# Moving the branch to a general path ahead of the last two row groups of a projection

## The chip, the cores and the metric

The kernel runs on one core of one Trainium2 chip. The core has five engines that each run their own list of instructions in order: TensorE (PE in the profile, with its weight loads as PEld), VectorE (DVE), ScalarE (ACT), GpSimd (POOL) and SyncE (SP), which here only issues transfers. Sixteen DMA engines move data between the chip's memory (HBM) and the core's on-chip memories, SBUF and, for the results of TensorE, PSUM with eight banks. Engines wait for one another through counters (semaphores). The metric is the device time of one execution in microseconds (us), the median of several runs; a profiled execution gives the trace.

## The reference

Causal attention over a sliding window of 64 positions, and a SwiGLU feed-forward block behind it:

```
q, k, v: (8 batches, 8 heads, 576 positions, 64)
scores = q @ k^T / 8;  kept where 0 <= pos_q - pos_k < 64, else -1e9
attn   = softmax(scores);  x = attn @ v      -> 4608 tokens of 512
g   = x @ w_gate;  val = x @ w_val           (512 -> 1536)
out = (silu(g) * val) @ w_out                (1536 -> 512), float32
```

## The kernel before, in words

The kernel computes in bfloat16 with float32 sums. It cuts the 4608 tokens into NT = 9 tiles of 512. Eight tiles are positions 0 to 511 of one batch each; the tile LAST = 7 collects positions 512 to 575 of all batches. The tile handled last, t = 8, is batch 7, tokens 4032 to 4543.

A tile goes through attention (scores, weights, totals, the mix with v, each with its helper), whose result is xT[t], transposed; then gate_value, twelve times, once for each 128 of the 1536 hidden features: eight products into two banks, SiLU on ScalarE, and a product on VectorE into hT[t] (line 467). hT[t] has shape 128 x 12 x 512: feature within a chunk, chunk, token. The projection takes a row group s, that is 128 of the 512 tokens, and sums twelve products over the chunks: `hT[t][:, c, P * s:P * s + P]` is the stationary operand and `wo[:, c, :]` the moving one (project_part, line 482). project_end copies the bank to a tile os_ and SP issues the transfer to the output. The loop over t puts the projection of tile t - 1 in among the attention of tile t. For the last tile it stands alone behind the loop (lines 986 to 988): row groups 0, 1 and 2 through project into banks 5, 7 and 4, and row group 3 through project_last, in two parts of 384 and 128 columns with a copy and a transfer each.

The fast path does not subtract the row maximum before the exponential. So it surveys its sums: fifty-six columns of `spread` hold totals and extents, survey (line 542) asks which lie within a bound, and tally (line 549) counts the partitions on which all do. Line 982 loads that count into a register of each engine. The If on line 989 then runs the general path where the count is below 128: general_attention once for each of 64 batch and head pairs, which keeps the maximum and writes x to a scratch tensor x_all in HBM, and general_ffn once for each 128 tokens, which reads x_all, computes the block anew and overwrites the output. Both issue their transfers on ScalarE's queue. Each engine takes the branch for itself, at its place in its list. In the run the count is 128: no instruction of lines 554 to 661 is in the trace.

The order of instructions on every engine is the order of the program text (a manual schedule). The framework adds the waits and the counters. Transfers issued by SP and ScalarE take eight counters in turn; in the trace they are 100, 103, 104, 105, 106, 107, 109 and 110. Where a branch does not run its body, its other arm adds to the counters what the body would have counted. Tiles of one tag share its buffers: os_ has four, and the tag hT of hpool has two.

```
    for s in range(3):
        project(NT - 1, s, bank[(5, 7, 4)[s]])
    project_last(NT - 1, 3)
    with tc.If(good < P, preferred_fallthrough_block=True):
```

Of the kernel before, what the change touches and what calls it, by code (L numbers as in the profile page):

```python
# [8 lines left out]
P = 128  # L9
FP32 = mybir.dt.float32  # L10
BF16 = mybir.dt.bfloat16
# [6 lines left out]
def kernel(  # L18
# [10 lines left out]
    nc = tc.nc  # L29
    S, D, H = 576, 64, 8  # L30
    NTOK, DFF, DM = 4608, 1536, 512
    NT = NTOK // 512
# [10 lines left out]
    hpool = ctx.enter_context(tc.tile_pool(name="hpool", bufs=2))  # L43
    ps = ctx.enter_context(tc.tile_pool(name="ps", bufs=1, space=PSUM))
    two = [ps.tile([P, 2, 512], FP32, name=f"two{i}") for i in range(2)]
    bank = [two[i][:, j] for i in range(2) for j in range(2)]
# [21 lines left out]
    scratch = ctx.enter_context(  # L68
        tc.tile_pool(name="scratch", bufs=1, space=bass.MemoryType.DRAM)
    )  # L70
    x_all = scratch.tile([H * D, NTOK], BF16, name="x_all")
    floor = cst.tile([P, 1], FP32, name="floor")
    LEAST, MOST = 2.0 ** -60, 2.0 ** 30
    columns_used = [0]
# [455 lines left out]
    def project_last(t, s):  # L530
        r0 = S * batch(t) + P * s
        os_ = fsb.tile([P, 512], FP32, name="os_", tag="os_", bufs=4)
        for f0, f1, o_ps in ((0, 384, bank[6]), (384, 512, bank[0])):
            for c in range(12):
                nc.tensor.matmul(  # L535
                    o_ps[:, 0:f1 - f0], hT[t][:, c, P * s:P * s + P], wo[:, c, f0:f1],
                    start=(c == 0), stop=(c == 11),
                )
            nc.vector.tensor_copy(os_[:, f0:f1], o_ps[:, 0:f1 - f0])
            nc.sync.dma_start(out[r0:r0 + P, f0:f1], os_[:, f0:f1])  # L540
# [13 lines left out]
    def general_attention(i):  # L554

        def rows(ap, lo, hi):
            return ap.rearrange("b h s d -> (b h) s d")[bass.ds(i, 1), lo:hi]

        plain, wide = {}, {}
        for n, src in (("q", q), ("k", k), ("v", v)):  # L560
            f = stage.tile([P, 6, D], FP32, name=n + "_g", tag=n, bufs=1 if n == "v" else 2)
            nc.gpsimd.memset(f[:], 0.0)
            lead = 0 if n == "q" else 64
            if lead:
                nc.scalar.dma_start(f[64:P, 0], rows(src, 0, 64).rearrange("o r d -> r (o d)"))
            else:
                nc.scalar.dma_start(f[0:64, 4], rows(src, 512, S).rearrange("o r d -> r (o d)"))
            c0 = lead // 64
            nc.scalar.dma_start(
                f[:, c0:c0 + 4], rows(src, lead, lead + 512).rearrange("o (c r) d -> r (o c) d", r=P)  # L570
            )
            plain[n] = epool.tile([P, 6, D], BF16, name=n + "_h", tag="both")
            nc.gpsimd.tensor_copy(plain[n][:], f[:])
        for n, b in (("q", 4), ("k", 5)):
            tp = bank[b].bitcast(BF16)
            for c in range(6):
                nc.tensor.transpose(tp[0:D, P * c:P * c + P], plain[n][:, c], identb[:])
            wide[n] = att.tile([P, 6 * P], BF16, name=n + "_w", tag="qT")
            nc.scalar.copy(wide[n][0:D], tp[0:D, 0:6 * P])
        W = P + 64  # L580
        s_ps = [two[c // 4][:, c % 4 // 2, c % 2 * W:c % 2 * W + W] for c in range(5)]
        for c in range(5):
            nc.tensor.matmul(
                s_ps[c], wide["q"][0:D, P * c:P * c + P], wide["k"][0:D, P * c:P * c + W]
            )
        s = room(2).rearrange("r a b -> r (a b)")[:, 0:5 * W].rearrange("r (c j) -> r c j", j=W)
        nc.scalar.activation(
            s[:, 0:4].rearrange("r (a c) j -> r a (c j)", a=2), two[0][:, :, 0:2 * W],
            AF.Copy, scale=0.125,
        )  # L590
        nc.scalar.activation(s[:, 4], s_ps[4], AF.Copy, scale=0.125)
        for sign, base in ((1, 64), (-1, -1)):
            nc.gpsimd.affine_select(
                out=s, in_=s, compare_op=ALU.is_ge, fill=-1e9,
                base=base, pattern=[[0, 5], [-sign, W]], channel_multiplier=sign,
            )
        nc.gpsimd.memset(s[:, 0, 0:64], -1e9)
        some = fsb.tile([P, 64], FP32, name="some", tag="fine", bufs=1)
        top, total = some[:, 0:5], some[:, 5:10]
        nc.vector.tensor_reduce(top, s, axis=mybir.AxisListType.X, op=ALU.max)  # L600
        nc.gpsimd.tensor_scalar(top, top, -1.0, 0.0, op0=ALU.mult, op1=ALU.add)
        for c in range(5):
            nc.scalar.activation(
                s[:, c], s[:, c], AF.Exp, bias=top[:, c:c + 1], accum_out=total[:, c:c + 1]
            )
        nc.gpsimd.tensor_scalar(total, total, 1.0, 1e-9, op0=ALU.mult, op1=ALU.add)
        nc.vector.reciprocal(total, total)
        e, p0, p1 = (t[:].rearrange("r s z -> r (s z)") for t in eb[0:3])
        e = e[:, 0:5 * W].rearrange("r (c j) -> r c j", j=W)
        nc.vector.tensor_mul(e, s, total.unsqueeze(2).to_broadcast([P, 5, W]))  # L610
        t0, t1 = bank[6].bitcast(BF16), bank[7].bitcast(BF16)
        for c in range(5):
            nc.tensor.transpose(t0[:, P * c:P * c + P], e[:, c, 0:P], identb[:])
            nc.tensor.transpose(t1[0:64, P * c:P * c + P], e[:, c, P:W], identb[:])
        nc.scalar.copy(p0[:, 0:5 * P], t0[:, 0:5 * P])
        nc.scalar.copy(p1[0:64, 0:5 * P], t1[0:64, 0:5 * P])
        o_ps = two[0][0:D].rearrange("r a b -> r (a b)")
        for c in range(5):
            cs = slice(P * c, P * c + P)
            nc.tensor.matmul(o_ps[:, cs], plain["v"][:, c], p0[:, cs], start=True, stop=False)  # L620
            nc.tensor.matmul(
                o_ps[:, cs], plain["v"][0:64, c + 1], p1[0:64, cs], start=False, stop=True
            )
        x_h = att.tile([P, S], BF16, name="x_h", tag="xT")
        nc.scalar.copy(x_h[0:D], o_ps[:, 0:S])
        nc.scalar.dma_start(
            x_all[bass.ds((i % H) * D, D), bass.ds((i // H) * S, S)], x_h[0:D]
        )

    def general_ffn(i):  # L630

        x_b = att.tile([P, 4, P], BF16, name="x_b", tag="xT")
        nc.scalar.dma_start(
            x_b[:], x_all[:, bass.ds(i * P, P)].rearrange("(c r) s -> r c s", r=P)
        )
        h_b = hpool.tile([P, DFF], BF16, name="h_b", tag="hT")
        h_t = hpool.tile([P, 12, P], BF16, name="h_t", tag="hT")
        for lo, hi, pair in ((0, 2, two), (2, 3, [bank[b].unsqueeze(1) for b in (4, 5)])):
            for w, ps_ in zip((wg, wv), pair):
                for f in range(lo, hi):  # L640
                    for c in range(4):
                        nc.tensor.matmul(
                            ps_[:, f - lo], x_b[:, c], w[:, c, 512 * f:512 * f + 512],
                            start=c == 0, stop=c == 3,
                        )
            sg, val = room(hi - lo), room(hi - lo)
            nc.scalar.activation(sg, pair[0][:], AF.Silu)
            nc.scalar.copy(val, pair[1][:])
            nc.gpsimd.tensor_mul(
                h_b[:, 512 * lo:512 * hi].rearrange("r (a f) -> r a f", f=512), sg, val  # L650
            )
        for b, c0 in ((6, 0), (7, 6)):
            tp = bank[b].bitcast(BF16)[:, 0:6 * P].rearrange("r (c s) -> r c s", s=P)
            for c in range(6):
                nc.tensor.transpose(tp[:, c], h_b[:, P * (c0 + c):P * (c0 + c) + P], identb[:])
            nc.scalar.copy(h_t[:, c0:c0 + 6], tp)
        for c in range(12):
            nc.tensor.matmul(bank[4], h_t[:, c], wo[:, c, :], start=c == 0, stop=c == 11)
        os_ = fsb.tile([P, 512], FP32, name="os_", tag="os_", bufs=4)
        nc.scalar.copy(os_[:], bank[4])  # L660
        nc.scalar.dma_start(out[bass.ds(i * P, P)], os_[:])

    def set_exp():
        nc.scalar.preload_act_table_set("natural_log_exp_and_others")
# [318 lines left out]
        count[0:1, 0:1], min_val=0, max_val=P,  # L983
        skip_runtime_bounds_check_because="a count of 128 partitions",
    )
    for s in range(3):
        project(NT - 1, s, bank[(5, 7, 4)[s]])
    project_last(NT - 1, 3)
    with tc.If(good < P, preferred_fallthrough_block=True):
        set_exp()  # L990
        with tc.For_i(0, 8 * H, 1) as b:
            general_attention(b)
        set_silu()
        with tc.For_i(0, NTOK // P, 1) as i:
            general_ffn(i)

# [1 line left out]
_INS = ['q', 'k', 'v', 'moe_w_gate', 'moe_w_val', 'moe_w_out']  # L998
# [26 lines left out]
```

## Time and profile before

| what | value |
|---|---|
| median of 3 runs | 323.33 us (323.15 to 324.28) |
| the profiled execution | 323.03 us |
| its span, first to last instruction | 321.3 us |
| granted TensorE clock over the span | 1.0 |
| TensorE, weight loads | 315.1 us (98%), 154.8 us (48%) |
| VectorE, ScalarE, GpSimd | 214.4, 208.7, 148.0 us |
| products of line 482, mean of one | 252, 379 ns |
| last copy of VectorE ends | 317.0 us |

The page of the profile counts as busy only what computes; register loads, branches, counter instructions and the issue of transfers are in the trace, with a q behind the engine's name (SPq, PEldq), and can be listed by the line that made them. The products of TensorE overlap: one of 512 columns lasts 379 ns, but the next starts 216 ns after it. "The chain" follows the work that ended last back to what released each step. The DMA view gives for any stretch the packets and their queue; the queues marked "instruction" carry the engines' own code.

### The profile page before, as it was taken

What the parts mean: (1) busy time and instruction counts of PE and PEld (TensorE: products, weight loads), DVE (VectorE), ACT (ScalarE), POOL (GpSimd) and SP (SyncE); (2) the same over time, 40 slices, a digit from 0 to 9 for tenths busy, and PEclk for the clock granted to TensorE, in tenths of its full rate; (3) what the DMA queues carried; (4) which work ended last, traced back from release to release, by engine and by line L of the source; (5) the groups of instructions that cost most, each with busy time, mean ns of one, the idle gap of its engine ahead of it and who ended that gap; (6) DMA issues with size and microseconds to landing.
All of it is one profiled execution on the core that took longest, in us unless ns stands there. A gap on an engine that the chain in (4) does not pass through costs nothing.

```text
span 321.3 us, 8212 instructions
## 1 busy us (share of the span) xinstructions
PE 315.1 (98%) x3298; PEld 154.8 (48%) x3298; DVE 214.4 (67%) x349; ACT 208.7 (65%) x327; POOL 148.0 (46%) x268
## 2 busy tenths in 40 slices
PE   8999999999999999999999999999999999999994
PEld 3544444445444644454445544554456444644442
DVE  4878846496676747684688657866785677744421
ACT  5967665768565875687467846694668565865500
POOL 4965656957557246741751099308665300000000
PEclk9999999999999999999999999999999999999999
DMA  7999999999799449974993379529997400021012
GB/s 251 204 196 198 207 147 229 201 194 132 153 193 181 49 114 179 194 79 106 162 199 41 80 115 116 65 62 143 181 185 100 107 0 0 4 92 43 0 44 92
DMA packets 83530, 40.45 MB, mean 126 GB/s; under 512 B 64161, under 2 KB 78753, under 8 KB 83489
## 3 DMA queue, kind: packets, MB, share of 16 engines
q0 software_dynamic: 51488, 22.59, 58.5%
q1 hardware_dynamic: 31456, 16.79, 22.7%
q8 instruction: 26, 0.43, 0.5%
q10 hardware_dynamic: 544, 0.52, 0.5%
q14 instruction: 16, 0.12, 0.1%
HBM read 53.02 MB, written 9.44 MB: 194 GB/s over the span
## 4 chain that ended last, share of the span: by engine, by line
PE 95%; ACT 2%; DMA 2%; ACTq 0%; DVE 0%; issue 0%
PE one L473 56%; PE one L482 17%; PE one L494 11%; PE two L293 3%; PE two L414 2%; PE one L449 2%; DMA k_f<-in_k_dram 2%; ACT eb L738 1%; PE two L336 1%; PE one L535 1%; PE two L449 1%; PE one L336 0%; ACT r L350 0%; ACT qk_b L724 0%; ACT r L353 0%; PE two L877 0%
## 5 line engine op out<-in xcount | busy, mean ns | idle before, releaser
L466 ACT ACTIVATE sg<-one 128x512 f32<-128x512 f32 x107 | 63.9, 597 | 80.5 <-PE one L473 65.5
L467 DVE TENSOR_TENSOR hT<-sg,one 128x512 bf16<-128x512 f32 x107 | 74.0, 692 | 57.5 <-PE one L473 53.8
L473 PE MATMUL one<-xT,wg 128*128 128x512 bf16 x416 | 106.8, 379 | 0.0
L473 PE MATMUL one<-xT,wv 128*128 128x512 bf16 x416 | 106.8, 379 | 0.0
L142 POOL DMA_DIRECT2D k_s<-in_k_dram x112 | 60.6, 570 | 26.5 <-DMA q_s<-in_q_dram 15.1
L473 PEld LDWEIGHTS <-wv 128*128 128x128 bf16 x416 | 40.7, 98 | 49.1
L473 PEld LDWEIGHTS <-wg 128*128 128x128 bf16 x416 | 40.6, 98 | 48.8
L482 PE MATMUL one<-wo,hT 128*128 128x512 bf16 x252 | 56.5, 379 | 0.0
L956 POOL COPY past<-xT 128x1 bf16<-128x1 bf16 x8 | 1.5, 192 | 88.1 <-DVE xT L430 88.1
L494 PE MATMUL one<-wo,hT 64*64 64x512 bf16 x672 | 40.0, 377 | 0.0
L482 PEld LDWEIGHTS <-hT 128*128 128x128 bf16 x252 | 23.8, 98 | 29.3 <-issue 2.0
L430 DVE TENSOR_TENSOR xT<-two,r 128x512 bf16<-128x512 f32 x34 | 21.2, 683 | 22.7 <-ACT r L353 22.7
L233 DVE STREAM_TRANSPOSE kT<-k_s 128x512 bf16<-128x512 bf16 x28 | 36.1, 1288 | 0.0
L753 ACT ACTIVATE eb<-eb 128x960 bf16<-128x960 bf16 (+1 forms) x32 | 32.0, 1001 | 0.0
L308 ACT ACTIVATE eb<-two 128x960 bf16<-128x960 f32 (+1 forms) x32 | 29.5, 974 | 3.0 <-PE two L293 2.9
L494 PEld LDWEIGHTS <-hT 64*64 64x64 bf16 x672 | 18.6, 107 | 13.7
L313 DVE TENSOR_TENSOR eb<-eb,mask 128x960 bf16<-128x960 bf16 (+1 forms) x32 | 21.0, 656 | 5.8 <-ACT eb L308 5.8
L223 DVE STREAM_TRANSPOSE qT<-q_s 128x512 bf16<-128x512 bf16 x32 | 22.2, 700 | 0.1
L353 ACT ACTIVATE r<-r 128x1024 f32<-128x1024 f32 (+1 forms) x20 | 19.2, 968 | 0.1
L318 DVE TENSOR_TENSOR both<-eb 128x512 bf16<-128x512 bf16 x32 | 13.6, 425 | 1.1
L107 POOL DMA_DIRECT2D q_s<-in_q_dram x24 | 13.1, 553 | 2.3 <-DMA v<-in_v_dram 1.3
L168 POOL DMA_DIRECT2D vb<-in_v_dram x16 | 11.1, 705 | 5.1 <-DMA wo<-in_moe_w_out_dram 3.5
(149 smaller groups left out, 272.9 us busy)
## 6 DMA issues: line engine op xcount, KB each, us to landing
k_s<-in_k_dram POOLq DMA_DIRECT2D x112, 56.0 KB, 5.0
q_s<-in_q_dram POOLq DMA_DIRECT2D x24, 248.0 KB, 6.0
v_f<-in_v_dram SPq DMA_DIRECT2D x40, 128.0 KB
wg<-in_moe_w_gate_dram POOLq DMA_DIRECT2D x5, 256.0 KB, 8.2
wv<-in_moe_w_val_dram POOLq DMA_DIRECT2D x5, 256.0 KB, 8.8
q_f<-in_q_dram SPq DMA_DIRECT2D x4, 256.0 KB
wo<-in_moe_w_out_dram POOLq DMA_DIRECT2D x2, 512.0 KB, 10.7
vb<-in_v_dram POOLq DMA_DIRECT2D x16, 64.0 KB, 6.2
```

Source lines behind the costliest of these rows:

```text
L142: nc.gpsimd.dma_start(k_s[p0:p0 + 32, g, :, 0:w], k[b, a:H:2, s:s + P].rearrange("u (r e) d -> r u (e d)", e=4) [:, :, 32 * c:32 * c + w],)
L223: nc.vector.transpose(queries[t][:, u, :].rearrange("r (e x) -> r e x", e=16), staged[t][0][:, u].rearrange("r (e d) -> r e d", d=D)[:, :, ...
L233: nc.vector.transpose(dst[:, u, :].rearrange("r (g x e) -> r g e x", g=4, e=4), k_s[:, :, u].rearrange("r g (e d) -> r g e d", d=D)[:, :, ...
L308: nc.scalar.activation(flat, s_ps[:].rearrange("r a b -> r (a b)")[:, 0:n], AF.Exp, scale=0.125)
L313: nc.vector.tensor_mul(flat, flat, mask[:].rearrange("r j c e y -> r (j c e y)")[:, 0:n])
L430: nc.vector.tensor_mul(x, o_ps, r)
L466: nc.scalar.activation(sg[:], g_ps[:], AF.Silu)
L467: nc.vector.tensor_mul(hT[t][:, m, :], sg[:], v_ps[:])
L473: nc.tensor.matmul(ps[:], w[:, c, P * m:P * m + P], xT[t][:, c, :], start=(c == 0), stop=(c == 3),)
L482: nc.tensor.matmul(o_ps[:], hT[t][:, c, P * s:P * s + P], wo[:, c, :], start=(c == 0), stop=(c == 11),)
L494: nc.tensor.matmul(tiles[s][half(y)], hT[t][half(x), c, r0:r0 + 64], wo[half(x), c, :], start=not back and c == 0, stop=bool(back) and c = ...
L753: nc.scalar.activation(flat, flat, AF.Copy, accum_out=extent())
```

## The change

The If moves up by two row groups. Ahead of it stay row groups 0 and 1 of the last tile; behind it come row group 2 through project and row group 3 through project_last. What they read, columns 256 to 511 of hT[NT - 1], must then hold the right values on either path, and so the general path no longer ends with the output alone:

- general_ffn takes its transposed hidden values h_t not as a tile of its own but as columns 384 to 511 of hT[NT - 1]. Before it overwrites them it copies them on ScalarE to columns 256 to 383. After the last two passes these hold the values of the last two groups of 128 tokens it handled.
- For these to be the tokens of row groups 2 and 3 (4288 to 4543), the groups are shifted by 64 tokens. x_all has 64 more columns; general_attention writes each batch 64 columns on, and once more its last 64 positions into columns 0 to 63, where the last batch's stay. general_ffn's group i is then tokens 128 i - 64 to 128 i + 63, wrapped round for i = 0, and its output goes out in two transfers of 64 rows.
- A pass of general_attention now issues eight transfers instead of seven, and one of general_ffn three instead of two. The tag hT is asked for one tile less.

```diff
-    x_all = scratch.tile([H * D, NTOK], BF16, name="x_all")
+    x_all = scratch.tile([H * D, NTOK + 64], BF16, name="x_all")
...
-        nc.scalar.dma_start(
-            x_all[bass.ds((i % H) * D, D), bass.ds((i // H) * S, S)], x_h[0:D]
-        )
+        row = (i % H) * D
+        nc.scalar.dma_start(x_all[bass.ds(row, D), bass.ds((i // H) * S + 64, S)], x_h[0:D])
+        nc.scalar.dma_start(x_all[bass.ds(row, D), 0:64], x_h[0:D, S - 64:S])
...
-        h_t = hpool.tile([P, 12, P], BF16, name="h_t", tag="hT")
+        h_t = hT[NT - 1][:, :, 384:512]
+        nc.scalar.copy(hT[NT - 1][:, :, 256:384], h_t)
...
-        nc.scalar.dma_start(out[bass.ds(i * P, P)], os_[:])
+        nc.scalar.dma_start(out[bass.ds((i * P + NTOK - 64) % NTOK, 64)], os_[0:64])
+        nc.scalar.dma_start(out[bass.ds(i * P, 64)], os_[64:P])
...
-    for s in range(3):
+    for s in range(2):
         project(NT - 1, s, bank[(5, 7, 4)[s]])
-    project_last(NT - 1, 3)
     with tc.If(good < P, preferred_fallthrough_block=True):
         set_exp()
-        with tc.For_i(0, 8 * H, 1) as b:
-            general_attention(b)
+        with tc.For_i(0, 8 * H, 1) as i:
+            general_attention(i)
         set_silu()
         with tc.For_i(0, NTOK // P, 1) as i:
             general_ffn(i)
+    project(NT - 1, 2, bank[4])
+    project_last(NT - 1, 3)
```

## The prediction

> **What bounds the kernel now.** The page comes first: its busy rows and the chain that ended last.
>
> ```profile
> span 321.3 us, 8212 instructions
> ...
> PE 315.1 (98%) x3298; PEld 154.8 (48%) x3298; DVE 214.4 (67%) x349; ACT 208.7 (65%) x327; POOL 148.0 (46%) x268
> ...
> PE 95%; ACT 2%; DMA 2%; ACTq 0%; DVE 0%; issue 0%
> ```
>
> TensorE (PE) is the bound nearly everywhere, at full granted clock. The change touches only what comes after the last SwiGLU value, so the chain in order of time, from 305 us on, is next.
>
> ```profile
> 306.29 7.77 PE one L482 x36
> 314.06 1.95 PE one L535 x12
> 316.01 0.68 PE two L535 x12
> 316.69 0.02 issue
> 316.71 0.29 DVE os__4707 L539
> ```
>
> PE runs without a hole to 316.69. VectorE's last copy ends at 317.0, yet the span ends at 321.3: 4.3 us of tail with no engine busy. What fills it is in the instructions of the If's line (989), in those of the kernel's end (1020), and in the DMA view from 318.2 to 318.4.
>
> ```profile
> L989 SPq EVENT_SEMAPHORE  x8: 17/17/17, 317.7 to 319.6; - x8
> L989 POOLq COMPARE_BRANCH  x1: 50/50/50, 306.0 to 306.0; - x1
> L989 ACTq COMPARE_BRANCH  x1: 50/50/50, 306.0 to 306.0; - x1
> L989 ACTq EVENT_SEMAPHORE  x1: 17/17/17, 306.5 to 306.5; - x1
> ...
> L989 PEldq COMPARE_BRANCH  x1: 236/236/236, 314.9 to 314.9; - x1
> L989 PEldq EVENT_SEMAPHORE  x1: 51/51/51, 316.7 to 316.7; - x1
> L989 DVEq COMPARE_BRANCH  x1: 72/72/72, 316.7 to 316.7; - x1
> L989 DVEq EVENT_SEMAPHORE  x1: 21/21/21, 317.3 to 317.3; - x1
> L989 SPq COMPARE_BRANCH  x1: 50/50/50, 317.5 to 317.5; - x1
> ```
>
> ```profile
> L1020 SPq EVENT_SEMAPHORE  x12: 28/28/28, 319.7 to 320.4; - x12
> L1020 SPq DRAIN  x2: 7/10/12, 320.4 to 320.5; - x2
> ```
>
> ```profile
> q14 instruction: 1, 0.01, 14.7%
> ```
>
> No engine waits at the branch itself. Behind the jump each has an instruction that waits until the engine's own earlier work is counted and then adds what the general path would have counted: one each on four engines, eight on SP, one for each counter of its transfers. PE branches at 314.888, while 17 products are still queued, and reaches its arm at 316.718, 0.043 after its last product's end at 316.675. SP stands in its arm until the last output has landed (its eighth wait passes at 319.636), runs twelve waits of the kernel's end 0.061 apart, and drains at 320.506; two rounds of all engines close the span.
>
> The DMA line is one 8 KB packet of code: 14.7% of 16 engines in 0.2 us is 0.47 us, from 318.207 to 318.678 on one DMA engine. Eight 512-byte packets of the last output stand behind it. Fifteen of that output's sixteen parts land by 318.71, the sixteenth at 319.62. The packet follows VectorE's jump: VectorE has run 124 instructions since the packet at 240.7 us, the step between its earlier ones (124, 126, 123), SP only 19 since its own at 292.7. ScalarE's and GpSimd's jumps have theirs too, at 307.06 and 307.09.
>
> **The change, part by part.** The profile after would start from the same 305 us: nothing ahead of the load of the count moves, and no instruction of lines 554 to 661 runs, so the larger scratch tensor, the shifted addresses, the two added transfers and the copy into hT cost nothing while the branch skips them. What cover there is: the skip itself; were the path taken, all would be paid.
>
> *The branch on PE.* Two row groups (24 products) now come ahead of it; behind it are 36 products, for which VectorE's last three copies and SP's last three transfers wait. The compare goes 17 products ahead as now, so its 0.236 us is covered by 17 x 0.216 = 3.7 us of queued products; uncovered it would add those 0.24. The arm's wait, though, stands between two products. The second row group's last product starts at 311.086 and ends at 311.465; the arm follows 0.043 later, at 311.508. From an arm to the next instruction the trace has 0.149 (PE, 316.718 to its drain at 316.867) and 0.075 (the start barrier's wait at 0.744 to the weight load at 0.819); from a weight load to its product 0.031 there and 0.005 at 4.9 us. The product then starts at 311.59 to 311.69 instead of 311.302: a hold of 0.29 to 0.39. Nothing hides it; I take 0.35, nearer the upper row, which is the same arm. Below: 0, if the add does not hold what follows. Above: the moved products read hT, which the general path writes on ScalarE, and a bank that ScalarE reads there, so PE must wait for ScalarE's add; that came at 306.5 and costs nothing. Should PE also wait for VectorE's add, that one comes 0.322 after the copy ending at 312.194 (as 317.327 after 317.005), at 312.52, and the hold is 1.3.
>
> [...]
>
> *The branch on VectorE.* Its arm comes at about 312.5 and the next copy at 314.43: 1.9 us of cover. Its code packet comes 0.88 after the arm (as 318.207 after 317.327), at about 313.4, on the second row group's output, and no longer on the last one. Gain: 319.62 - 318.71 = 0.91. Lower end 0, if some engine's code packet still falls there.
>
> *The branch on SP.* Queued behind its arm are the transfers of the third and fourth row groups. The arm passes when the second group's output has landed: 314.35, or 0.91 later if the code packet delays that one as it did the last, and three more adds at about 0.08: 314.6 to 315.5. The third group's copy ends at 314.785 + 0.35 = 315.1, its transfer takes 0.37 to issue, and the fourth's first is due at 316.6 + 0.35. At the worst SP is free at 315.9, 1 us early: no cost, and what is late next is only the third group's landing.
>
> *The end of SP.* Eight adds leave the tail; the one that mattered stood behind the landing. Further, the transfers take eight counters in turn: the first row group 104 and 105, the second 106, third 107, last 109 and 110, and the end waits in the order 100, 103 to 107, 109, 110. The general path issued 7 + 2 transfers a pass and will issue 8 + 3. Counted on from 106, these take 107 to 106 and 107 to 110, so the third group gets 100, the last 103 and 104. The seven waits ahead of that for 104 then run before the landing, and five follow: 0.016 + 5 x 0.061 + two drains of 0.065 = 0.45 from landing to the last drain, where it was 320.506 - 319.62 = 0.89. Gain 0.44; ends: 0, if the order makes all twelve follow again, and 0.89 - 0.15 = 0.74, if only the drains follow.
>
> *GpSimd and ScalarE* branch at 306.0 as before, with nothing behind.
>
> **Sum.** 0.35 - 0.91 - 0.44 = -1.00. The profiled execution took 323.03 (span 321.33 and 1.70 around it) and would take 322.0; the median of the runs is 0.30 above it, at 323.33, and would come to 322.3. With the ends of the terms together the median lies between 323.33 - 0.91 - 0.74 = 321.7 and 323.33 + 1.3 = 324.6.
>
> **The rivals.**
>
> 1. *Half the gain is missing.* Code still lands on the last output, or PE waits for VectorE's add. For it: VectorE's code boundary is known only by counting. Time: 323.33 + 0.35 - 0.44 = 323.2, or 323.33 + 1.3 - 1.35 = 323.3.
>
> 2. *Slower: PE waits for SP's add.* The general path writes the output by DMA, from tiles of the same pool as the last copies, and its inputs reach on-chip tiles by DMA. If one of the moved products inherits such a counter, PE restarts at 314.67 to 315.6 instead of 311.30: a hold of 3.4 to 4.3. Time 323.33 - 1.35 + 3.4 = 325.4, up to 326.3. It decides from a hold of 1.35 + 1.6 = 3.0 us on. Against: what the moved products touch (hT, wo, three banks) no DMA of the general path touches; the copies behind them may wait, with cover.
>
> 3. *Slower too: PE lacks the code behind the jump.* A packet of PE's code is 0.43 MB / 26, for 6596 recorded instructions at 65 bytes some 250 of them. The general path has 37 + 48 products with a weight load each, 170 instructions and the loops' own: a little less than one packet, so the target is at most in the next packet. From a branch to the packet that follows it is 1.06 us (306.0 to 307.06), and PE's packet at 314.01 lasted 0.97: 2.0 for one, if the compare no longer runs ahead. Time 323.33 - 1.35 + 0.35 + 2.0 = 324.3, and 326.4 if the code behind the arm needs another. Against: PE's code packet came before its branch, none after it, and ScalarE, GpSimd and VectorE passed arms before their packets came. [...]
>
> 4. *Faster than the bound: no hold at all.* The adds let PE through and all waits but the drains precede the landing: 323.33 - 0.91 - 0.74 = 321.7, at the edge. For it: nothing but the lower ends.
>
> **How the numbers follow.** The forecast's own case gets 0.60, rival 1 0.15, rival 2 0.07, rival 3 0.11 (half of it at 324.3), rival 4 0.07. Half a per cent is 1.6 us, about what a measurement of this kernel can tell from no change. Faster by more: rival 4 and 0.04 of the forecast's own, 0.11. Slower: rival 2 and the worse half of rival 3, 0.13. The rest, 0.76, is within. The range runs from rival 4's 321.7 to just above rival 3's single fetch, 324.4, and leaves out the slow ends and part of rival 4. I predict 322.3 us.
>
> **What would show it.** Right: one hole of about 0.35 us in PE between the second and third row groups; the If's instructions of VectorE at about 312.5 and of SP ending before 315.5; no code packet among the last output's, whose sixteen parts land within 0.2 us; about 0.45 from that landing to the drain. Wrong: a hole over 1.3 us, PE's code packet inside it, SP issuing the fourth row group's first part later than VectorE's copy by more than 0.1, or a straggling last landing.

## The result, and the profile after

| | before | after |
|---|---|---|
| median (22 runs each) | 323.4 us | 322.6 us |
| ratio, 95% interval | | 0.9978 (0.9968 to 0.9989) |
| profiled execution, its span | 323.03, 321.3 us | 322.44, 320.6 us |

The change is worth 0.8 us by the medians, 0.4 to 1.0 by the interval of the ratio: 0.2%, forecast 0.3%. The single times spread over 1.7 us (before) and 2.3 us (after), so the terms are read from the trace instead, on a clock that starts behind that spread: VectorE's conversion of the count (line 552), which every engine then loads for the branch. From there to SP's last drain ahead of the closing rounds it is 305.245 to 320.506 before, 15.26 us, and 305.491 to 319.794 after, 14.30 us. So the changed part took 0.96 us less, and this profiled execution had come to it 0.25 us later.

The chain in order of time, after, from 306 us:

```profile
311.82 0.04 issue
311.86 2.75 PE one L482 x12
314.61 1.95 PE one L535 x12
316.56 0.68 PE two L535 x12
317.25 0.02 issue
317.27 0.29 DVE os__4888 L539
```

The chain now begins at 311.82, because there the profile shows nothing that TensorE (PE) waited for ("issue"). The last product of the second row group starts at 311.332, and the next one at 311.860 where it would have been due at 311.548: a hole of 0.31 us. The If's instructions, after (now line 990):

```profile
L990 SPq EVENT_SEMAPHORE  x8: 17/17/17, 313.1 to 314.9; - x8
...
L990 PEldq COMPARE_BRANCH  x1: 366/366/366, 307.7 to 307.7; - x1
L990 PEldq EVENT_SEMAPHORE  x1: 51/51/51, 311.8 to 311.8; - x1
L990 DVEq COMPARE_BRANCH  x1: 72/72/72, 311.8 to 311.8; - x1
L990 DVEq EVENT_SEMAPHORE  x1: 21/21/21, 312.5 to 312.5; - x1
L990 SPq COMPARE_BRANCH  x1: 50/50/50, 312.9 to 312.9; - x1
```

TensorE ends its compare 3.7 us before the second row group's last product ends (308.049 to 311.711) and reaches its arm at 311.754, 0.043 after its last product's end; the weight load follows 0.076 later. SP's eight adds lie between the second and third outputs and are over at 314.9; the third row group's copy ends at 315.395 and its transfer is issued at 315.422.

The DMA view of the whole tail, after, from 317.7 us to the end of the span, has one queue, where the tail of before also had a packet of code:

```profile
q1 hardware_dynamic: 288, 0.26, 26.0%
```

The sixteen parts of the last output land between 319.15 and 319.36; before, fifteen lay between 318.56 and 318.71 and the last at 319.62. VectorE's code packet is now at 312.93, on the second output. Last, SP in the kernel's end (now line 1023), from that landing on:

```profile
L1023 SPq EVENT_SEMAPHORE  x6: 28/28/28, 319.4 to 319.7; - x6
L1023 SPq DRAIN  x2: 7/7/7, 319.7 to 319.8; - x2
```

Six waits, the first of them the landing's own and five behind it. Before, the landing's own wait was the last of the eight in the branch's arm, and all twelve of the kernel's end stood behind it.

### The profile page after: what moved, and what is told of

It is laid out like the page before. It is cut to its first block, busy times and chain, and to the rows that moved or that the text cites. A ratio compares the mean times of both kernels' runs of the same rounds, so it can differ in the third digit from the quotient of the medians.

```text
span 320.6 us, 8214 instructions
## 1 busy us (share of the span) xinstructions
PE 315.5 (98%) x3298; PEld 154.8 (48%) x3298; DVE 214.4 (67%) x349; ACT 208.7 (65%) x327; POOL 147.4 (46%) x268
```

## The experiments

My theory was the sum of the prediction: a hold of TensorE by its own arm, against a code packet that no longer delays the last output, and waits that now run before the landing. The main rival was simpler: a branch costs something at the end, and moving it up takes that cost out of the tail, so that the place decides. All stretches below come from the trace of each kernel's profiled execution, in us; "count" is the conversion of line 552, and each ratio is to executions of the kernel before that ran beside that kernel.

| kernel | count to last product's end | VectorE's last copy to landing | landing to SP's drain | count to drain | median, ratio to before (95%) |
|---|---|---|---|---|---|
| before | 11.43 | 2.62 | 0.89 | 15.26 | 323.4 to 323.7 |
| after | 11.74 | 1.80 | 0.44 | 14.30 | 322.6, 0.9978 (0.9968 to 0.9989) |
| end_code_moved | 11.43 | 1.70 | 0.88 | 14.34 | 322.72, 0.9977 (0.9967 to 0.9987) |
| two_ahead_last_counter | 11.74 | 1.75 | 0.17 | 13.99 | 322.32, 0.9959 (0.9944 to 0.9975) |
| the same again | 11.74 | 1.75 | 0.17 | 13.99 | 322.46, 0.9966 (0.9954 to 0.9978) |
| no_branch | 11.43 | 1.72 | 0.14 | 13.62 | 322.55, 0.9966 (0.9953 to 0.9979) |
| the same again | 11.43 | 1.73 | 0.15 | 13.63 | 322.42, 0.9956 (0.9943 to 0.9969) |
| second_if_pe | 12.05 | 1.80 | 0.44 | 14.62 | 323.0, 0.9984 (0.9973 to 0.9996) |
| second_if_no_pe | 11.74 | 1.80 | 0.44 | 14.31 | 322.87, 0.9977 (0.9966 to 0.9988) |
| four_ahead | 11.85 | 1.80 | 0.44 | 14.43 | 322.74, 0.9976 (0.9964 to 0.9989) |

In every row the last product's end and the end of VectorE's last copy are 0.33 apart.

**The code packet alone: the branch stays at the end.** Twenty one-column memsets on VectorE, in its waits of the last tile.

```diff
+    spare = cst.tile([P, 1], FP32, name="spare")
...
         for m in range(12):
             gate_value(t, m)
+            if t == NT - 1 and m < 10:
+                for _ in range(2):
+                    nc.vector.memset(spare[:], 0.0)
```

> The kernel before, with its If at the end, and twenty one-column memsets on VectorE between its products of the last tile, where it waits about 1 us for each bank. They move VectorE's code on, so that its code boundary is crossed some 14 instructions ahead of the branch and the jump stays inside one code packet. Theory (a code packet on the last output, worth about 0.9): no code packet after 317 us, one near 308; the last output's sixteen parts land within 0.2 us; from the count's conversion (line 552) to SP's drain 14.4 us instead of 15.26; median about 0.9 under the kernel before, 322.5, with the branch where it was. Rival (the gain comes from where the branch stands): 15.3 us, and a median like that of the kernel before.

The DMA view of this kernel from 310.5 to 311.5 us, and then from 317 us to the end of the span:

```profile
q14 instruction: 1, 0.01, 3.0%
```

```profile
q1 hardware_dynamic: 289, 0.26, 19.6%
```

Twenty instructions of VectorE moved the packet from the tail to 310.70, later than the 308 that I expected, but out of the tail; it also shows whose code it is. The last output's parts landed within 0.17 us, the stretch from the last copy to the landing fell by 0.91, and the two other stretches of the table stayed. The median fell by as much as with the change itself, with the branch where it was. So the main rival is out: this gain does not need the move. Beside this kernel the change itself is 0.04 us better from count to drain (14.30 against 14.34). What the move adds, 0.44 less behind the landing, is nearly used up by the hold of 0.31 and by 0.09 more from copy to landing.

**The counters alone.** The changed kernel; five transfers of the general path, none of which runs, become ten.

```diff
-            nc.scalar.dma_start(
-                f[:, c0:c0 + 4], rows(src, lead, lead + 512).rearrange("o (c r) d -> r (o c) d", r=P)
-            )
+            for h in range(2):
+                c, r0 = c0 + 2 * h, lead + 256 * h
+                nc.scalar.dma_start(
+                    f[:, c:c + 2], rows(src, r0, r0 + 256).rearrange("o (c r) d -> r (o c) d", r=P)
+                )
...
-        nc.scalar.dma_start(
-            x_b[:], x_all[:, bass.ds(i * P, P)].rearrange("(c r) s -> r c s", r=P)
-        )
+        x_in = x_all[:, bass.ds(i * P, P)].rearrange("(c r) s -> r c s", r=P)
+        for h in range(2):
+            nc.scalar.dma_start(x_b[:, 2 * h:2 * h + 2], x_in[:, 2 * h:2 * h + 2])
...
-        nc.scalar.dma_start(out[bass.ds(i * P, 64)], os_[64:P])
+        nc.scalar.dma_start(out[bass.ds(i * P, 32)], os_[64:96])
+        nc.scalar.dma_start(out[bass.ds(i * P + 32, 32)], os_[96:P])
```

> The changed kernel, with five of the general path's transfers split in two (three of a pass of general_attention, two of one of general_ffn), none of which runs. The eight counters then go on so that the last three outputs take 107, 109 and 110 instead of 100, 103 and 104. Theory (the waits of the kernel's end that stand behind the last landing): five waits of 0.061 move ahead of the landing, so that 0.15 instead of 0.43 lies between it and SP's drain; 14.0 us instead of 14.30 from the count's conversion to the drain; median about 0.3 under the changed kernel, 322.3. Rival (transfers that never run cannot matter): 14.3 us and 322.6.

> The changed kernel with five transfers of the general path split, once more, beside the floor on one chip. Theory: 14.0 us from the count's conversion to SP's drain and a median 1.2 to 1.3 below the kernel before, ratio 0.996. If the first median was luck, the ratio is 0.998 like the changed kernel's.

SP in the kernel's end (here line 1026), from the landing at 319.90 on:

```profile
L1026 SPq DRAIN  x2: 7/7/7, 320.0 to 320.1; - x2
L1026 SPq EVENT_SEMAPHORE  x1: 28/28/28, 319.9 to 319.9; - x1
```

One wait and the drains are left: 0.165 from landing to drain instead of 0.44, in both profiled executions, and 13.99 in all. Both medians lie below that of the changed kernel; the intervals overlap that of the changed kernel, so that the waits are gone is shown by the trace and not by them. This version has the lowest time of those that keep the general path.

**The floor.** The If and the general path are taken out of the changed kernel, twice.

> The changed kernel without the If and so without the general path, which is left out altogether: the floor of what the branch costs. Theory: no hold of TensorE (0.31 back), no code packet on the last output, only drains behind the landing: 13.7 us from the count's conversion to SP's drain, median 321.8. If the branch costs something that the three terms do not hold (the compare, the adds, the code to be passed over), it falls below 13.5 us.

> The kernel without the If and the general path once more (the general path is left out altogether), because its median of 322.55 lay 0.7 above what its stretch behind the count gives. Theory (that run's excess came from ahead of the count, where the profiled execution lost 1.2 us to a late key transfer for tile 2): 13.6 us behind the count again, median 321.9, 0.4 below the version with the last counter. Rival (without the general path something ahead of the count is slower for good): 13.6 us behind the count, median 322.5 again, and the same late transfer.

SP in the kernel's end of the first (here line 1016), from the landing at 319.98 on:

```profile
L1016 SPq DRAIN  x2: 7/7/7, 320.1 to 320.1; - x2
L1016 SPq EVENT_SEMAPHORE  x1: 28/28/28, 320.0 to 320.0; - x1
```

Behind the count both executions agree with the theory: 13.62 and 13.63 against 15.26 - 0.91 - 0.74 = 13.61. So the code packet and the waits are the whole price of the branch at the end, to some 0.02 us; where the change puts it, the price is 14.30 - 13.62 = 0.68, made of the hold (0.31), 0.07 from copy to landing and 0.30 of waits.

The medians, 322.55 and 322.42, miss the 321.8 and 321.9 that I expected. The late key transfer did not come back in the second profiled execution, so it does not explain the second median. The record shows where the excess lies: each execution has its time and its span, and what the time holds outside the span is 2.14 and 2.13 us here (medians of 7 and 5 executions), but 1.73 for the kernel before beside each (22 and 25). The spans alone, in the median, fell by 1.4 and 1.7, around the 1.64 of the tail; 0.4 us was lost outside them. What fills that time the traces do not show, so it stays open.

**What holds TensorE.** A second If on the same count between the last two row groups, once with a small product in its body, `marker`, as shown, and once with `set_exp()` in its place, which has none.

```diff
     project(NT - 1, 2, bank[4])
+    with tc.If(good < P, preferred_fallthrough_block=True):
+        marker(5, 0)
     project_last(NT - 1, 3)
```

> The changed kernel with a second If on the same count between the third and fourth row groups, whose body is one 16-column product into a bank no longer in use. Theory (TensorE is held by its arm's wait for its own products): a second hole of about 0.3 us on TensorE, 14.6 us from the count's conversion to SP's drain, median 322.9. Rival (what held TensorE was the code to be fetched once): no second hole, 14.3 us.

> The changed kernel with a second If on the same count between the third and fourth row groups, whose body only loads ScalarE's table and has no product. Every engine still compares and jumps, but TensorE has nothing to add and so no wait in its arm. Theory (the arm's wait holds TensorE, the compare and the jump do not): one hole of 0.31 between row groups two and three and none at the second branch; 14.3 us from the count's conversion to SP's drain, as in the changed kernel. Rival (each branch stops TensorE): a second hole of 0.2 to 0.3, 14.6 us, as with a product in the body.

The second If's instructions on TensorE and the chain of work around it, with the product and then without:

```profile
L998 PEldq COMPARE_BRANCH  x1: 219/219/219, 312.7 to 312.7; - x1
L998 PEldq EVENT_SEMAPHORE  x1: 51/51/51, 315.5 to 315.5; - x1
```

```profile
315.52 0.04 issue
315.57 1.46 PE one L535 x8
```

```profile
L998 PEldq COMPARE_BRANCH  x1: 216/216/216, 312.2 to 312.2; - x1
```

```profile
312.09 2.75 PE one L482 x12
314.84 1.95 PE one L535 x12
```

Both compare for 0.22 us. Only the first has an arm with a wait, and only the first has a second hole: its products at the seam start 0.528 apart, exactly as at the first branch, 0.31 more than the usual 0.216; the other goes through without one. So the compare and the jump cost TensorE nothing here, where products are queued behind them (11.74 to the last product's end, as in the changed kernel), and the wait for its own last product costs 0.31 each time.

**The place of the branch.** The If straight behind the load of the count.

```diff
-    for s in range(2):
-        project(NT - 1, s, bank[(5, 7, 4)[s]])
     with tc.If(good < P, preferred_fallthrough_block=True):
...
-    project(NT - 1, 2, bank[4])
+    for s in range(3):
+        project(NT - 1, s, bank[(5, 7, 4)[s]])
     project_last(NT - 1, 3)
```

> The If straight behind the load of the count, ahead of all four row groups; the general path then leaves only the values of two of the four groups, so it would not be whole if it were taken, but it is not taken. Theory (the price on TensorE is its wait for its own last product, wherever the branch stands): one hole of about 0.31 before the first row group, at most 0.2 more because the compare no longer runs ahead of queued products; code packets at once behind it; the same counters as in the changed kernel; 14.3 to 14.5 us from the count's conversion to SP's drain. Rival (the branch is cheap only behind 3 us of queued products): the code behind the jump comes late, a hole of 2 us or more and 16 us.

TensorE in order of time, and the DMA view from 307.8 to 308.05:

```profile
307.30 7.93 PE L482 MATMUL one<-wo,hT 128*128 128x512 bf16 x36 [0.26 <-PEq L988]
```

```profile
q8 instruction: 1, 0.02, 38.7%
```

The hold is 0.42 (11.85 - 11.43), because the compare of 0.35 now follows the load of the count with little left in the queue: the last product ends at 307.04, the compare only at 307.14. The rest is the changed kernel's to 0.01. TensorE starts again at 307.30, and its next packet of code only begins at 307.91: it did not wait for code behind the jump even without 3 us of products ahead.

## Why the prediction was right

The median came out at 322.6 for 322.3, in the range, and the term by term sum at -0.96 for -1.00. The three terms are the ones that the trace shows. That the sum is nearer than its terms is luck in part: a hold taken 0.04 too long makes up for some of a gain taken 0.09 too large.

- *The hold of TensorE*, 0.35 taken, 0.31 measured. The row from the start barrier, 0.075, was the better of the two: from arm to weight load it is 0.076. The compare took 0.366 instead of 0.236 and began 17 products ahead, so its cover held.
- *The code packet*, 0.91, and 0.91 in the kernel that takes it away alone. In the changed kernel the stretch from copy to landing gained 0.82. What gave 0.06 of it back I had put at nothing: behind the branch the wait for TensorE's count stands in an instruction of its own ahead of the fourth group's first copy (it ends at 316.609), and that copy starts 0.08 after its product is counted (316.575 to 316.652) instead of 0.02 (316.020 to 316.043). SP's two last issues stand 0.42 apart in both kernels, so the last begins 0.10 instead of 0.05 after its copy. Another 0.04 lies between that issue and its landing (1.69, against 1.65 in end_code_moved); why is not shown.
- *The waits behind the landing*, 0.44, measured 0.45. Five follow the landing's own, as worked out; six stand ahead of it, not the seven of the prediction, which changes nothing in the sum.
- *SP's arm* between the outputs cost nothing, as worked out: the third group's issue comes 0.03 after its copy (315.395 to 315.422). VectorE's code packet came 0.45 after its arm, not 0.88, at 312.93, and the second output's last part landed only 0.19 behind the others instead of up to 0.91.
- *Rival 1* fell with the tail free of code and with TensorE's restart at 311.83, ahead of VectorE's add at 312.48; *rival 2* with the same restart, 1.3 us ahead of SP's first add and 3.1 ahead of its last. *Rival 3* fell with four_ahead, where TensorE starts again at 307.30 and its next packet of code begins at 307.91; no run here shows TensorE waiting for code behind a jump, and none jumps over more code than the general path's. *Rival 4* fell with the hole of 0.31 and the five waits of the trace after; the two kernels that have a second If show what makes the hole.
- The forecast gain of 1.00 lies at the upper edge of the interval (0.4 to 1.0). Of the 0.3 between forecast and median, 0.07 is the kernel before, which came out at 323.4 over 22 executions instead of 323.33 over 3. Most of the rest fits a step that the sum took without a reason: it left the 1.70 around the span as it was. In the 22 executions after, this time outside the span is 1.78 to 2.01, in the median 1.92. For the kernel before it is 1.73 where it is on record (22 and 25 executions beside the experiments). What fills it is not shown.

## What to carry to other kernels

A branch that was not taken was not free here where it stood between two products: TensorE finished all it had before it added, 0.31 us in the changed kernel and again at the second If of second_if_pe; in second_if_no_pe a body without products avoided that second hole. At the end of a kernel look at which transfer lands last, at what moves beside it and at what runs behind the landing: here a code packet, 0.91 us, and up to twelve waits in a fixed order, 0.74 us. Both were moved by instructions that do no work or never run (twenty memsets; five split transfers, with which one wait was left), so a gain of some tenths of a microsecond beside a moved statement need not come from the statement. The time of an execution also holds something outside the span, which here differed between kernels by up to 0.4 us, so a sum over the trace is to be compared with the trace first.

## What the runs showed of the hardware that I had not expected

A code packet was traffic here: one 8 KB packet of VectorE's code, 0.47 us on one DMA engine, put off the end of the whole kernel by 0.91, with eight small packets of the last output behind it.

The spread of the single times has its own places ahead of the count. Against the execution of before, the other profiled ones lose 0 to 0.7 us ahead of the first SwiGLU value, up to 1.25 at tile 2 and up to 0.5 at tile 7. For tile 2 the trace shows where the time goes: VectorE's waits in no_branch (its first execution) from 60 to 70 us, against none of the kind before.

```profile
DVE kT L233 <- DMA vb<-in_v_dram: 1.4, 1, 1.4
```

The turn (transpose) of tile 2's keys starts at 65.08 instead of 63.61, and the products of two features behind it come late. The view puts the wait down to a transfer of vb, the values; the turn itself reads the keys, k_s, so which transfer was late is not settled. What makes that transfer land late in one execution and not in another was not tried.
